# A weight decoding shared out anew: 16-bit copies on ScalarE, the first rescaling on GpSimd

## The chip, the cores and the metric

The kernel runs on one core of a Trainium2 chip. Its time is the device time of one launch in microseconds (us), the median of several runs; less is better. A core has five engines with queues of their own: TensorE (matrix products, PE in the rows), VectorE (DVE), ScalarE (ACT), GpSimd (POOL) and SyncE (SP, which here issues the DMA transfers). Each engine takes its instructions strictly in the order in which the program lists them; between engines they wait for each other by semaphores.

## The reference

Attention with normalized queries and keys, and then a feed-forward part. Inputs and the weights are drawn in NumPy: q, k, v are float32, the weights come to the kernel as float64.

```python
def _attn_ref(q, k, v, g_q, g_k):            # q, k, v: (8, 12, 448, 64)
    q_n, k_n = rmsnorm(q, g_q), rmsnorm(k, g_k)
    scores = matmul(q_n, k_n.T) / sqrt(64)
    attn = softmax(scores)                   # with 1e-9 added to the sum
    return matmul(attn, v)

def _moe_ref(x, w_in, w_out):                # x: (3584, 768), w_in: 768 x 2048
    h = x @ w_in
    g = h * np.cos(h)
    return g @ w_out                         # w_out: 2048 x 768
```

## The kernel before

The kernel has two parts. The first does all the attention, two heads at a time (48 units `u`, six of them to each of the 8 batches), and between the units' instructions the products `h = x @ w_in` of the batches already done. The second part does the last products of this kind, the cosine and the product with `w_out`. All products are made in float32 precision from a high and a low part of each operand; the first six units alone are "plain", that is, they use float32 products without such parts.

The 16 blocks of `w_in` (one for each 128 of the 2048 hidden columns, 128x768 numbers each) arrive as float64, 768 KB each, by DMA (`w_load`, L254). The chip doesn't compute in float64, so each is decoded in place. The 64-bit numbers are seen as pairs of 32-bit words; the upper word (`up`) holds sign, exponent and the first 20 bits of the mantissa, the lower word the other 32, of which float32 still takes 3. `decode` (L259 to L270) does this in four steps:

- step 0, ScalarE (L263): the upper words, read as float32, are multiplied by 2 to the power of -112 into a buffer `f`, which corrects the exponent;
- step 1, ScalarE (L266): the highest byte of each lower word is copied over the lowest byte of the upper word;
- step 2, VectorE (L268): the upper word is shifted right arithmetically by 5, and sign and three lowest bits are kept;
- step 3, VectorE (L270): `f` is shifted left by 3 as an integer, and combined with the upper word by "or".

Then ScalarE makes the high part (`w_high`, L280) and VectorE the low part, in two halves (`w_low`, L285). For the buffer `f` the blocks take turns between two places, `wf` and `aq`. A block's decoding needs the place that the block before the last has left.

The weights `w_out` go the same way in 32 quarters of 128x384 (`v_fetch`, `v_decode`), between about 180 and 860 us. Their seven combinations are stored in DRAM for the second part.

Other names in the rows: `score_plain` (L551) and `score` (L567) make the scores `S`; `rowmin` (L571, VectorE) scales them and finds their extreme; `expo` (L579, ScalarE) makes the probabilities `P`; `transp` (L613 to L622) transposes them on TensorE into PSUM `PT`; `pt_copy` (L668, L670) copies `PT` to SBUF for the plain units, `pt_high` and `pt_low` (L636, L643, L645) make its high and low part for the others; `av` (L660, L662) and `av_plain` (L678 to L688) multiply by v. On GpSimd are the powers for the norms (`st_pow`, L398, L399), the scaling of keys (`k_norm`, L473, L476) and queries (`q_scale`, L492), the low parts of both (`k_low`, L482, `q_low`, L498), v's parts (L522, L526), the division by the sum (`x_norm`, L717) and the low part of x (`x_split`, L728). `ffn1` (L744 to L746) makes the first product of the feed-forward part.

The order of the instructions isn't written by hand. Each piece of work is given by `add` an engine, a cost and a due time, and what it reads and writes. `Plan.order` then walks through time with these costs: an engine that is free takes, of the pieces that are ready, the one due first. The resulting list is emitted as it is. The due times are corrected by tables of numbers: `SHIFT` (by function and stage), `PAIR` (by unit), `BEGIN` (the earliest start of loads) and some terms in the number of the block. After that `hold` moves the pieces named in `YIELD` behind a key's normalization where one follows within 4 us, in the first 60 us.

Of the kernel before, what the change touches and what calls it, by code (L numbers as in the profile page):

```python
# [13 lines left out]
U8 = mybir.dt.uint8  # L14
# [11 lines left out]
class Plan:  # L26
# [123 lines left out]
    YIELD, AHEAD, WITHIN, UNTIL = ("x_norm", "w_low"), "k_norm", 4.0, 60.0  # L150
# [20 lines left out]
def tile_attention_moe(  # L171
# [14 lines left out]
    NP = NU // B  # L186
    NQT = 7
# [158 lines left out]
    kboth, qlow = {}, [apool.tile([128, 768], F32R, tag="E0", name="E0", bufs=1)]  # L346
# [18 lines left out]
    def e_clear(i):  # L365
        if i:
            qlow.append(apool.tile([128, 768], F32R, tag="E1", name="E1", bufs=1))
# [85 lines left out]
    def rkb(u):  # L453
        return (qtwo[u % 2][:, :S] if u < NP else kboth[u % 2][:, S:]).bitcast(F32)

# [3 lines left out]
    def rk_load(u):  # L459
        if u < NP + 2:  # L460
# [10 lines left out]
    def k_norm(u):  # L471
        if u >= NP:
# [11 lines left out]
    def q_plain(u):  # L484
        return q6[:, u]
# [4 lines left out]
    def q_scale(u):  # L490
        q = q_plain(u) if u < NP else qd
        nc.gpsimd.tensor_scalar(q, q, gsc[u < NP], 0.0, op0=ALU.mult, op1=ALU.add)  # L492

# [35 lines left out]
    def place(u, n):  # L529
        i = 7 * min(u, NP) + (n if u < NP else 0)  # L530
        if u < NP:
            return ("ph", i // 4) if i % 4 == 3 else ("S", 3 * (i // 4) + i % 4)
        return ("S", i - i // 4 + 7 * (u - NP) + n)

    NSP = 7 * NP // 4
# [72 lines left out]
    def transp(u, kc, part, last):  # L608
# [5 lines left out]
        else:  # L614
# [4 lines left out]
            c, n = (k - 64, 128) if u < NP else (k, 64)  # L619
# [215 lines left out]
    def y_store(b, oc, src):  # L835
# [5 lines left out]
        "av": (5.3, 39.33, 0.0), "av3": (-13.83, 15.47, 0.0), "av_plain": (0.0, 0.0, 10.94),  # L841
        "d_place": (7.71, -0.4, 0.0), "e_clear": (2.06, 0.0, 0.0), "e_place": (-13.2, 0.0, 0.0),
        "expo": (7.95, 14.26, -11.58), "ffn1": (-3.18, -2.89, 0.0), "g_fold": (0.0, 0.0, 3.13),
        "g_load": (0.0, 0.0, 0.98), "h_both": (-29.07, 0.0, 0.0), "h_out": (-14.91, 5.31, 0.0),
        "h_store": (-0.09, 0.0, 0.0), "k_high": (7.68, 8.19, 0.0), "k_load": (0.0, 0.0, 1.22),
        "k_low": (33.26, 1.74, 0.0), "k_norm": (45.02, 0.0, -0.54), "kn_copy": (0.0, 0.0, -13.33),
        "kn_load": (0.0, 0.0, -45.16), "kn_norm": (0.0, 0.0, -20.32), "kn_pow": (0.0, 0.0, 29.13),
        "kn_reduce": (0.0, 0.0, -2.77), "kn_square": (0.0, 0.0, -6.31), "kn_turn": (0.0, 0.0, 1.63),
        "kq_load": (-17.42, -14.74, 0.0), "m_place": (-18.39, 4.08, 0.0), "pt_copy0": (0.0, 0.0, -3.9),
        "pt_copy1": (0.0, 0.0, -44.97), "pt_high0": (-25.09, -5.18, 0.0), "pt_high1": (-9.32, -33.28, 0.0),  # L850
        "pt_low0": (-20.85, 10.99, 0.0), "pt_low1": (-5.79, -41.16, 0.0), "q_high": (-79.7, 2.11, 0.0),
        "q_load": (0.0, 0.0, 5.21), "q_low": (-2.0, 3.7, 0.0), "q_scale": (-57.44, -11.45, -3.1),
# [12 lines left out]
    }
    PAIR = (18.33, 10.11, -12.21, 0.63, 7.01, 13.7, -4.94, -21.21, -1.78, 0.0, -39.42, -0.16)
# [487 lines left out]
```

## Time and profile before

| | |
|---|---|
| median of 3 runs | 1362.52 us (1362.02 to 1363.71) |
| the profiled execution, time | 1365.0 us |
| its span, first to last instruction | 1363.2 us |
| TensorE busy | 1339.7 us, 98% |
| VectorE, ScalarE, GpSimd busy | 74%, 72%, 42% |
| mean granted clock of TensorE | 0.996 |

Rows of the profile give an engine, a line of the kernel, an operation with its output and inputs, and times. In a timeline a row is the start, the duration, the engine, the line, the operation and its operands with their shapes, and in brackets how long the engine stood idle before it, and what released it. PE's durations overlap, since products are pipelined: the distance between two starts tells what one costs. A wait that has several causes is put down to the one that came last.

### The profile page before, as it was taken

The numbers are of one execution on the slowest core, as the hardware profiler recorded it, in microseconds if no ns is written. First come the engines' busy times: TensorE is split into PE (matmuls) and PEld (weight loads), VectorE is DVE, ScalarE is ACT, GpSimd is POOL, SyncE is SP. The second block draws the span as 40 slices with busy tenths as digits, with TensorE's granted clock in tenths as the row PEclk, the third lists the DMA queues.
The fourth block names the chain that finished last, engine by engine and source line by source line (L and its number), as shares of the span: only waits on it lengthen the run. The fifth ranks groups of instructions, "written<-read, shape, count | busy, mean of one in ns | idle before, by whom it ended". The sixth has DMA issues, their size and how long they took to land.

```text
span 1363.2 us, 21477 instructions
## 1 busy us (share of the span) xinstructions
PE 1339.7 (98%) x6998; PEld 1173.4 (86%) x6998; DVE 1013.0 (74%) x1795; ACT 977.6 (72%) x1920; POOL 579.1 (42%) x522
## 2 busy tenths in 40 slices
PE   6998999999999999999999999999999999999998
PEld 3447888988989899899898889999999999999998
DVE  5988887677777767677767776518889889889743
ACT  7999988787887888787887787646566366366321
POOL 4576657676765866765765675310000000000000
PEclk9998999999999999999999999999999999999999
DMA  6998879889898898898888878248989369369334
GB/s 209 263 286 221 178 192 236 227 240 245 237 234 219 216 245 222 212 256 227 215 221 229 219 208 225 88 176 278 332 287 311 111 246 315 107 246 316 104 113 153
DMA packets 149472, 302.19 MB, mean 222 GB/s; under 512 B 34368, under 2 KB 83088, under 8 KB 149360
## 3 DMA queue, kind: packets, MB, share of 16 engines
q1 hardware_dynamic: 149360, 300.83, 76.8%
q8 instruction: 55, 0.90, 0.3%
q14 instruction: 57, 0.47, 0.1%
HBM read 193.99 MB, written 62.73 MB: 188 GB/s over the span
## 4 chain that ended last, share of the span: by engine, by line
PE 87%; ACT 5%; DVE 3%; POOL 2%; issue 2%; DMA 1%; SPq 0%; ACTq 0%; POOLq 0%; DVEq 0%
PE y L819 10%; PE y L818 10%; PE y L820 10%; PE ph L744 9%; PE ph L745 9%; PE ph L746 9%; PE S L567 8%; PE PT L613 7%; PE O L660 5%; PE O L662 3%; ACT P L579 1%; PE y L746 1%; PE y L744 1%; PE y L745 1%; PE PT L618 1%
## 5 line engine op out<-in xcount | busy, mean ns | idle before, releaser
L571 DVE TENSOR_SCALAR_CACHE_REDUCE S<-S,r 128x448 f32<-128x448 f32 x336 | 224.8, 686 | 59.4 <-PE S L567 49.6
L744 PE MATMUL ph<-xs,wi 128*128 128x448 f32 x660 | 250.7, 380 | 0.2 <-ACT hbuf L762 0.2
L819 PE MATMUL y<-g,wo 128*128 128x448 f32 x672 | 245.4, 365 | 0.0
L818 PE MATMUL y<-g,wo 128*128 128x448 f32 x672 | 245.4, 365 | 0.0
L820 PE MATMUL y<-g,wo 128*128 128x448 f32 x672 | 245.4, 365 | 0.0
L745 PE MATMUL ph<-xs,wi 128*128 128x448 f32 x660 | 242.2, 367 | 0.0
L746 PE MATMUL ph<-xs,wi 128*128 128x448 f32 x660 | 241.4, 366 | 0.0
L579 ACT ACTIVATE P<-S,sm 128x448 f32<-128x448 f32 x336 | 214.4, 644 | 26.2 <-DVE S L571 23.7
L800 ACT CAST g<-gq 128x896 fp32r<-128x896 f32 x112 | 105.7, 943 | 172.8 <-PE y L820 172.3
L636 ACT CAST hi<-PT 128x512 fp32r<-128x512 f32 (+1 forms) x336 | 172.5, 538 | 73.1 <-PE PT L620 42.9
L643 DVE TENSOR_TENSOR lo<-PT,hi 128x512 fp32r<-128x512 f32 x252 | 151.4, 617 | 49.3 <-ACT hi L636 48.7
L798 DVE TENSOR_TENSOR g<-gq,g 128x896 fp32r<-128x896 f32 x112 | 122.0, 1089 | 61.5 <-ACT g L800 61.1
L613 PEld LDWEIGHTS PT<-ident,P 128*128 128x128 f32 x1008 | 120.7, 140 | 37.0 <-ACT hi L670 6.0
L613 PE MATMUL PT<-ident,P 128*128 128x128 f32 x1008 | 146.2, 274 | 1.8 <-DVE lo L643 1.5
L744 PEld LDWEIGHTS ph<-xs,wi 128*128 128x128 f32 x660 | 124.4, 188 | 13.9 <-ACT hbuf L762 1.4
L819 PEld LDWEIGHTS y<-g,wo 128*128 128x128 f32 x672 | 126.2, 188 | 10.0
L820 PEld LDWEIGHTS y<-g,wo 128*128 128x128 f32 x672 | 126.2, 188 | 10.0
L818 PEld LDWEIGHTS y<-g,wo 128*128 128x128 f32 x672 | 126.2, 188 | 10.0
L746 PEld LDWEIGHTS ph<-xs,wi 128*128 128x128 f32 x660 | 124.2, 188 | 10.7
L745 PEld LDWEIGHTS ph<-xs,wi 128*128 128x128 f32 x660 | 124.7, 189 | 8.7
L399 POOL TENSOR_TENSOR r<-r,nhalf 128x14 f32<-128x14 f32 (+1 forms) x48 | 122.6, 2554 | 4.0
L660 PE MATMUL O<-hi,vs 128*128 128x448 f32 x336 | 118.7, 370 | 0.0
(125 smaller groups left out, 2588.4 us busy)
## 6 DMA issues: line engine op xcount, KB each, us to landing
wo<-wo_d SPq DMA_DIRECT2D x152, 384.0 KB
gq<-h_d SPq DMA_DIRECT2D x64, 448.0 KB
h_d<-hbuf SPq DMA_DIRECT2D x54, 448.0 KB
wo_d<-ao SPq DMA_DIRECT2D x56, 384.0 KB
sd<-sd SPq DMA_DIRECT2D x46, 448.0 KB
kq<-kq SPq DMA_DIRECT2D x42, 480.0 KB
D<-qhi SPq DMA_DIRECT2D x84, 192.0 KB
raw<-w_in SPq DMA_DIRECT2D x16, 768.0 KB
```

The costliest lines, as they stand in the source:

```text
L571: nc.vector.tensor_scalar(d["S", t][:, :S], d["S", t][:, :S], d["r"][:, t : t + 1], None, op0=ALU.mult, op1=ALU.min, accum_out=d["sm"][:, ...
L579: nc.scalar.activation(p_rows(u, t), d.pop(("S", t))[:, :S], AF.Exp, bias=sm[:, 1, t : t + 1], scale=-1.0, accum_out=sm[:, 2, t : t + 1],)
L613: nc.tensor.transpose(pt[part][:, i * 128 : i * 128 + 128], p_rows(u, t)[:, c : c + 128], ident)
L636: nc.scalar.copy(hi if kc < 3 else hi[:64], pt_rows(u, kc, part))
L643: nc.vector.tensor_tensor(lo, src, hi.bitcast(F32), ALU.subtract)
L660: nc.tensor.matmul(O, st, d["hi", kc][:, HEADS[hh]], start=(kc == 0), stop=(kc == 3))
L744: nc.tensor.matmul(ph[:, :S], whi, x2[:, 0, :], start=(cc == 0), stop=False)
L745: nc.tensor.matmul(ph[:, :S], whi, x2[:, 1, :], start=False, stop=False)
L746: nc.tensor.matmul(ph[:, :S], wlo, x2[:, 0, :], start=False, stop=(cc == NCC - 1))
L818: nc.tensor.matmul(y, whi, hi[:, e], start=first and e == 0, stop=False, **more)
L819: nc.tensor.matmul(y, whi, lo[:, e], start=False, stop=False, **more)
L820: nc.tensor.matmul(y, wlo, hi[:, e], start=False, stop=last and e == NG - 1, **more)
```

## The change

- Step 1 of the decoding copies 16 bits for 8: the upper half of the lower word over the lower half of the upper word. Step 2 shifts by 13 instead of 5. This holds for both kinds of weights.
- Step 0 of `w_in`'s sixteen blocks goes from ScalarE to GpSimd (`w_rebias`, a product with 2 to the power of -112 and a sum with 0). For `w_out` step 0 stays on ScalarE.
- The costs that the planner assumes for step 3 and for `w_low` are changed (1.27 to 1.0, 0.53 to 0.6), and `w_low` no longer stands in `YIELD`.
- All the numbers in `SHIFT`, `PAIR` and `BEGIN` are new. New terms by number of block: -0.494 for -0.33 (`w_in`), 19.58 + 25.488 for 2.55 + 25.482 (`w_out`).
- A constant `NF` = 6 takes the place of `NP` = 6 and of literal numbers where the plain units are meant; the values are the same.

```diff
-    YIELD, AHEAD, WITHIN, UNTIL = ("x_norm", "w_low"), "k_norm", 4.0, 60.0
+    YIELD, AHEAD, WITHIN, UNTIL = ("x_norm",), "k_norm", 4.0, 60.0
...
         elif step == 1:
-            by = st.bitcast(U8).rearrange("p (n t) -> p n t", t=8)
-            nc.scalar.copy(by[:, :, 4], by[:, :, 3])
+            words = st.bitcast(U16).rearrange("p (n t) -> p n t", t=4)
+            nc.scalar.copy(words[:, :, 2], words[:, :, 1])
         elif step == 2:
-            nc.vector.tensor_scalar(up, up, 5, SIGN_LOW, op0=ALU.arith_shift_right, op1=ALU.bitwise_and)
+            nc.vector.tensor_scalar(up, up, 13, SIGN_LOW, op0=ALU.arith_shift_right, op1=ALU.bitwise_and)
...
+    def w_rebias(fc):
+        wfl[fc] = w_flat(fc)
+        up = raw[fc].bitcast(F32).rearrange("p (n t) -> p n t", t=2)[:, :, 1]
+        nc.gpsimd.tensor_scalar(wfl[fc], up, REBIAS, 0.0, op0=ALU.mult, op1=ALU.add)
+
     def w_decode(fc, step):
-        if step == 0:
-            wfl[fc] = w_flat(fc)
         decode(raw[fc], wfl[fc], step)
...
     SHIFT = {
...
-        "v_sum": (1.69, 0.0, 0.0), "w_decode": (70.22, 0.0, 0.0), "w_high": (3.68, 0.0, 0.0),
-        "w_load": (-3.56, 0.0, 0.0), "w_low": (2.76, 0.0, 0.0), "x_half": (-1.22, 1.78, 0.0),
...
+        "v_sum": (-17.09, 0.0, 0.0), "w_decode": (38.64, 0.0, 0.0), "w_load": (3.43, 0.0, 0.0),
+        "w_low": (7.04, 0.0, 0.0), "w_rebias": (2.77, 0.0, 0.0), "x_half": (7.15, -12.73, 0.0),
...
-    BEGIN = {"v_load": -5.46, "q_load": 4.31, "v_fetch": -9.59, "st_load": -5.63, "w_load": 12.81, "k_load": 10.48, "kq_load": -37.77, "v_plain": -2.91}
+    BEGIN = {"v_load": -9.1, "q_load": 4.47, "v_fetch": -39.58, "st_load": -4.95, "w_load": 12.86, "k_load": 15.5, "kq_load": -73.61, "v_plain": -0.99}
...
-        if name in ("w_load", "w_decode", "w_high", "w_low"):
-            due += -0.33 * first
+        if name in ("w_load", "w_rebias", "w_decode", "w_high", "w_low"):
+            due += -0.494 * first
...
-            late = BEGIN.get(name0, 0.0) + (0.075 * first if name0 == "w_load" else 0.0)
+            late = BEGIN.get(name0, 0.0) + (-0.001 * first if name0 == "w_load" else 0.0)
...
-            for step, eng, cost in ((0, ACT, 0.84), (1, ACT, 0.84), (2, DVE, 0.74), (3, DVE, 1.27)):
+            add(POOL, 1.0, d - 8.0, w_rebias, fc, r=[w], w=[f])
+            for step, eng, cost in ((1, ACT, 0.84), (2, DVE, 0.74), (3, DVE, 1.0)):
                 add(eng, cost, d - 8.0 + step, w_decode, fc, step,
-                    r=[w] if step in (0, 3) else [], w=[f] if step in (0, 3) else [w])
+                    r=[w] if step == 3 else [], w=[f if step == 3 else w])
...
-            add(DVE, 0.53, d, w_low, fc, hf, nc.vector, r=[f, w], w=[("wlo", fc, hf)])
+            add(DVE, 0.6, d, w_low, fc, hf, nc.vector, r=[f, w], w=[("wlo", fc, hf)])
```

## Rows read from the trace of the kernel before

**Rows 1.** The page's first part: busy time, share of the span, instructions, by engine

```profile
PE 1339.7 (98%) x6998; PEld 1173.4 (86%) x6998; DVE 1013.0 (74%) x1795; ACT 977.6 (72%) x1920; POOL 579.1 (42%) x522
```

**Rows 2.** Stretches: us, busy PE, PEld, DVE, ACT, POOL, then clock, DMA share, GB/s

```profile
100.00:110.00 10.00, 10.00 (x52) 6.72 (x51) 7.82 (x19) 9.70 (x20) 9.64 (x9) 1.00 1.05 294
110.00:120.00 10.00, 6.19 (x28) 4.77 (x28) 10.00 (x18) 9.56 (x20) 6.35 (x7) 0.79 1.08 255
...
20.00:180.00 160.00, 151.85 (x736) 97.89 (x737) 140.64 (x294) 150.13 (x295) 99.79 (x84) 0.98 0.89 237
...
260.00:1000.00 740.00, 739.61 (x4033) 668.24 (x4032) 521.78 (x1056) 564.16 (x1235) 413.76 (x374) 1.00 0.83 227
```

**Rows 3.** Waits of TensorE, 0 to 20 us: total us, times, longest

```profile
PE PT L438 <- DVE kq L433: 8.0, 1, 8.0
```

**Rows 4.** Waits of TensorE, 20 to 260 us

```profile
PE PT L618 <- DVE lo L643: 2.7, 1, 2.7
PE S L567 <- ACT P L579: 2.6, 3, 1.1
PE O L678 <- ACT hi L670: 2.1, 2, 1.1
PE PT L613 <- DVE lo L643: 1.5, 2, 0.8
PE S L551 <- ACT P L579: 1.1, 1, 1.1
```

**Rows 5.** Timeline of TensorE: start, us, line, operation, idle before and releaser

```profile
69.52 1.02 PE L551 MATMUL S<-km,q 128*128 128x448 f32 x2 [1.13 <-ACT P L579]
...
107.53 0.37 PE L744 MATMUL ph<-xs,wi 128*128 128x448 f32 x1
107.73 0.37 PE L745 MATMUL ph<-xs,wi 128*128 128x448 f32 x1
...
117.04 0.90 PE L618 MATMUL PT<-ident,P 128*128 128x128 f32 x3 [2.72 <-DVE lo L643]
...
118.70 0.57 PE L567 MATMUL S<-M,D 128*128 128x448 f32 x1
...
122.44 0.43 PE L745 MATMUL ph<-xs,wi 128*128 128x448 f32 x1
```

**Rows 6.** Timeline of ScalarE, 66 to 69 us

```profile
66.11 0.92 ACT L263 ACTIVATE aq<-raw 128x768 f32<-128x768 f32 x1 [1.16 <-issue]
67.06 1.96 ACT L266 COPY raw<-raw 128x768 uint8<-128x768 uint8 x1
```

**Rows 7.** Timeline of VectorE, at 63 and 107 us

```profile
63.40 0.55 DVE L285 TENSOR_TENSOR wi<-aq,wi 128x384 fp32r<-128x384 f32 x1
...
107.75 0.88 DVE L268 TENSOR_SCALAR raw<-raw 128x768 int32<-128x768 int32 x1 [1.45 <-ACT raw L266]
```

**Rows 8.** Tile raw: count, ns least/median/most, first and last start

```profile
L266 ACT COPY raw<-raw x16: 1907/1980/2091, 26.9 to 174.6; 128x768 uint8<-128x768 uint8 x16
...
L263 ACT ACTIVATE wf<-raw x8: 895/912/939, 25.5 to 165.3; 128x768 f32<-128x768 f32 x8
```

**Rows 9.** Tile rawo, a quarter of w_out

```profile
L266 ACT COPY rawo<-rawo x32: 1063/1080/1128, 190.4 to 860.6; 128x384 uint8<-128x384 uint8 x32
```

**Rows 10.** GpSimd by line and shape, 20 to 260 us: busy us, mean ns, idle before

```profile
L492 POOL TENSOR_SCALAR kq<-kq,gs 128x512 f32<-128x512 f32 x11 | 9.0, 814 | 6.9 <-DMA kq<-kq 6.9
L522 POOL TENSOR_SCALAR vs<-vd 128x512 fp32r<-128x512 f32 x10 | 6.3, 635 | 10.9 <-PE O L660 9.4 <-DMA vd<-v 1.5
L398 POOL TENSOR_SCALAR r<-r 128x14 f32<-128x14 f32 x15 | 4.7, 316 | 39.8 <-DVE r L393 39.6
```

**Rows 11.** All engines by line and shape, 0 to 200 us: w_low

```profile
L285 DVE TENSOR_TENSOR wi<-aq,wi 128x384 fp32r<-128x384 f32 x16 | 12.2, 786 | 0.4 <-ACT wi L280 0.3
L285 DVE TENSOR_TENSOR wi<-wf,wi 128x384 fp32r<-128x384 f32 x16 | 11.8, 769 | 0.6 <-ACT wi L280 0.6
```

More of the change, by code (lines that the diff above doesn't have):

```diff
@@ L13 @@
 I32 = mybir.dt.int32
-U8 = mybir.dt.uint8
+U16 = mybir.dt.uint16
 AF = mybir.ActivationFunctionType
@@ L186, in tile_attention_moe @@
     NP = NU // B
+    NF = 6
     NQT = 7
@@ L345, in tile_attention_moe @@
     KHOME = (0, 1, 2, 3, 4, 2)
-    kboth, qlow = {}, [apool.tile([128, 768], F32R, tag="E0", name="E0", bufs=1)]
+    kboth, qlow = {}, {}
     kq = apool.tile([128, S + 512], F32, tag="kq", name="kq", bufs=1)
@@ L365, in e_clear @@
     def e_clear(i):
-        if i:
-            qlow.append(apool.tile([128, 768], F32R, tag="E1", name="E1", bufs=1))
+        i = (NF + i) % 2
+        qlow[i] = apool.tile([128, 768], F32R, tag=f"E{i}", name=f"E{i}", bufs=1)
         nc.vector.tensor_scalar(
@@ L490, in q_scale @@
     def q_scale(u):
-        q = q_plain(u) if u < NP else qd
-        nc.gpsimd.tensor_scalar(q, q, gsc[u < NP], 0.0, op0=ALU.mult, op1=ALU.add)
+        q = q_plain(u) if u < NF else qd
+        nc.gpsimd.tensor_scalar(q, q, gsc[u < NF], 0.0, op0=ALU.mult, op1=ALU.add)
     def q_high(u):
@@ L529, in place @@
     def place(u, n):
-        i = 7 * min(u, NP) + (n if u < NP else 0)
-        if u < NP:
+        i = 7 * min(u, NF) + (n if u < NF else 0)
+        if u < NF:
             return ("ph", i // 4) if i % 4 == 3 else ("S", 3 * (i // 4) + i % 4)
-        return ("S", i - i // 4 + 7 * (u - NP) + n)
-    NSP = 7 * NP // 4
+        return ("S", i - i // 4 + 7 * (u - NF) + n)
+    NSP = 7 * NF // 4
     def score_plain(u, j):
@@ new lines, in tile_attention_moe @@
+        "ffn1": (-0.45, -3.23, 0.0), "g_load": (0.0, 0.0, 2.04), "h_both": (-14.26, 5.1, 0.0),
+        "h_out": (-12.49, 20.6, 0.0), "h_store": (2.07, 0.0, 0.0), "k_high": (10.35, 8.91, 0.0),
+        "k_low": (0.0, 11.42, 0.0), "k_norm": (58.53, 12.98, 2.31), "kn_copy": (0.0, 0.0, -0.84),
+        "kn_load": (0.0, 0.0, -28.91), "kn_norm": (0.0, 0.0, -0.93), "kn_pow": (0.0, 0.0, -0.07),
+        "kn_reduce": (0.0, 0.0, -3.51), "kn_square": (0.0, 0.0, -6.43), "kn_turn": (0.0, 0.0, 1.16),
+        "kq_load": (-20.41, -9.87, 0.0), "m_place": (27.69, 12.35, 0.0), "pt_copy0": (0.0, 0.0, -25.15),
@@ new lines, in tile_attention_moe @@
+        "pt_copy1": (0.0, 0.0, -67.76), "pt_high0": (-79.14, 41.7, 0.0), "pt_high1": (-6.74, -88.69, 0.0),
+        "pt_low0": (-24.23, 14.64, 0.0), "pt_low1": (27.75, 0.0, 0.0), "q_high": (-26.14, -6.02, 0.0),
+        "q_load": (0.0, 0.0, -0.09), "q_low": (-21.14, 2.75, 0.0), "q_scale": (-15.34, -4.21, 0.0),
+        "rk_load": (-17.86, 46.7, 0.0), "rk_spread": (0.0, 0.0, -3.79), "rowmin": (29.01, 67.9, 39.75),
+        "rs_copy": (5.99, 2.21, 3.92), "rs_load": (-3.46, 2.74, -26.9), "rs_store": (-13.25, 0.0, 4.69),
@@ new lines, in tile_attention_moe @@
+        "rsum": (5.13, -0.28, -0.33), "score": (0.0, -1.1, 0.0), "score_plain": (0.0, 0.0, -0.81),
+        "st_load": (8.97, 2.87, -1.4), "st_pow": (-19.93, 0.0, -1.56), "st_reduce": (37.79, -10.99, 16.99),
+        "st_square": (-0.1, -2.26, -2.95), "st_store": (15.14, 61.57, 3.04), "transp0": (-17.17, -38.32, -35.38),
+        "transp1": (3.55, -11.36, 0.0), "v_decode": (-43.76, 0.0, 0.0), "v_fetch": (-1.76, 0.0, 0.0),
+        "v_high": (0.0, 12.8, 0.0), "v_load": (-26.43, 2.23, 0.0), "v_low": (-91.11, -3.63, 0.0),
@@ L875, in add @@
         elif name[:2] not in ("w_", "v_", "e_") or name in ("v_load", "v_high", "v_low", "v_plain", "e_place"):
-            stage = 2 if first < NP else int(first < NP + 3)
+            stage = 2 if first < NF else int(first < NF + 3)
         if name in ("pt_low", "pt_high", "pt_copy", "transp"):
@@ L881, in add @@
         due += SHIFT.get(name, (0.0,) * 3)[stage]
-        if name in ("w_load", "w_decode", "w_high", "w_low"):
-            due += -0.33 * first
+        if name in ("w_load", "w_rebias", "w_decode", "w_high", "w_low"):
+            due += -0.494 * first
         if name in ("ffn1", "h_out", "h_store", "h_both") and not first:
-            due += -0.23 * args[1]
+            due += -0.328 * args[1]
         if name in ("v_fetch", "v_decode", "v_sum", "v_split", "v_store"):
-            due += 2.55 + 25.482 * first
+            due += 19.58 + 25.488 * first
         other = ("w_load", "w_decode", "w_high", "w_low", "v_fetch", "v_decode", "v_sum", "v_split", "v_store", "e_clear")
@@ L990, in prepare @@
             add(SP, ISS, D0 - 34, kq_load, u, w=kd + qd, kb=480.0, start=D0 - 40)
-        add(SP, ISS, D0 - 45, st_load, u, w=sd, kb=224.0 if turned else 448.0, start=0.0 if u < NP else D0 - 60)
+        add(SP, ISS, D0 - 45, st_load, u, w=sd, kb=224.0 if turned else 448.0, start=0.0 if u < NF else D0 - 60)
         if plain:
@@ L1164, in tile_attention_moe @@
             for i in range(RING["E"]):
-                add(DVE, 0.56, 24.0 + 45 * i, e_clear, i, w=[("E0", i)] + [("km", 4)] * i + [("E", NP + i)], start=20.0)
+                add(DVE, 0.56, 24.0 + 45 * i, e_clear, i, w=[("E0", i)] + [("km", 4)] * (i * (NF > 5)) + [("E", NF + i)], start=20.0)
         multiply(b, NFC if b < B - 1 else NEAR)
```

47 lines of the change are left out of this document (15 added, 32 removed).

## Prediction

> **What bounds the kernel now.** I began with the busy shares of the whole span: TensorE is busy 1339.7 us of 1363.2, 98% [rows 1]. A change on the other engines can therefore give back at most the 23.5 us in which TensorE is idle, and whatever it loses to a lower clock. Next I read the stretches, to see where those 23.5 us lie. From 260 to 1000 us TensorE is busy 739.61 of 740 us [rows 2]. That stage is closed: work saved there on another engine can't show. From 20 to 180 us TensorE is busy 151.85 of 160 us, while ScalarE is busy 150.13, VectorE 140.64 and GpSimd 99.79 [rows 2]. So the place to look is the first 260 us, and in it two engines stand almost as full as TensorE.
>
> TensorE's own waits from 20 to 260 us name the culprits: 2.6 + 2.1 + 1.1 = 5.8 us end with ScalarE (exponentials and PSUM copies), and 2.7 + 1.5 = 4.2 us end with VectorE's low part of the probabilities: 10.0 us in all [rows 4]. The opening 8.0 us, in which TensorE waits for the first normalized k, are outside this [rows 3]. The last few microseconds, the output store behind the last product, are untouched too.
>
> One of those waits costs more than itself. After the 2.72 us wait that ends at 117.04, ten matmuls begin between 118.70 and 122.44, 0.374 us apart, against 0.20 at 107.53 [rows 5]; the mean granted clock of 110 to 120 us is 0.79 [rows 2], so part of this stretch ran at the lower level, 1.2 GHz. It lasts about 5.4 us (117.04 to 122.44), of which 5.4 x (1 - 0.20/0.374) = 2.5 us are lost. What could be removed in all between 20 and 260 us is then 10.0 + 2.5 = 12.5 us.
>
> Last I read what stood on ScalarE ahead of such a wait. The exponential for which TensorE stands still until 69.52 [rows 5] came directly behind a rescaling (66.11, 0.92 us) and a byte copy (67.06, 1.96 us) [rows 6]. Three further waits on ScalarE have the same pair, or one of the two, a few instructions ahead of them: those that end near 32, 90 and 114 us. The 2.72 us wait goes the same way around a corner: VectorE stood idle 1.45 us for the byte copy at 107.75, with the two-part subtraction for which TensorE waited still queued behind [rows 7].
>
> **The change part by part.**
>
> *The rescaling leaves ScalarE.* Sixteen of 0.91 us [rows 8]: 16 x 0.91 = 14.6 us less between 25 and 175 us. ScalarE goes from 150.1 to about 135.5 of 160 us.
>
> *The copy moves 16 bits for 8.* The byte copy takes 1.98 us for 768 elements, over twice the float32 rescaling of the same count and the same 8-byte step on its input (0.91) [rows 8], and the 384-element copy takes 1.08 [rows 9]. No row shows a 16-bit copy. Upper bound: it stays at 1.98, if what is slow is a store of part of a word. Lower bound: 0.9, if only single bytes are slow. I take 0.95, since all wider rows of ScalarE lie there; that would save 16 x 1.03 = 16.5 us in the first stage, and nothing at the upper bound. The Trainium skill (ScalarE: Activation LUTs, section What ACT_TABLE_LOAD costs) gives 186 ns + 0.833 ns per element for every function, float32 and bf16 alike, which would be an estimated 0.83 us here. The float32 row is near it, the byte row is not, so the page has no word on bytes, and by it the saving would be 18.4 us instead of 16.5.
>
> The 32 later copies (384 elements) would save up to 32 x 0.55 = 17.6 us of ScalarE after 180 us. All but the first few lie in the stage in which TensorE waits for nothing, so I cost them at zero; what covers them is the full TensorE of [rows 2].
>
> *GpSimd takes the rescaling.* The nearest rows: one-input operations on 128x512 take 0.81 (q scaled) or 0.64 us (v copied), on 128x14 0.32 [rows 10]. Scaled from 512 to 768 elements: 0.64 x 1.5 = 0.96 and 0.81 x 1.5 = 1.2. The 8-byte step on the input has no row on this engine; if it doubled the cost, 2.4. I take 1.1, so 16 x 1.1 = 17.6 us more, GpSimd from 99.8 to 117 of 160 us. Most of GpSimd's idle time in there is waiting for VectorE's reductions, so the total fits. Not so near 100 to 110 us, where it is busy 9.64 of 10 [rows 2].
>
> *A new wait.* The 16-bit copy overwrites what GpSimd reads, so on ScalarE it now waits for GpSimd's rescaling. Behind it in ScalarE's queue are the exponentials and the PSUM copies, on which TensorE waits at once. Where GpSimd is on time it costs nothing; where it is late it costs up to one rescaling, 1.1 us. A rescaling in turn waits for the load and for the buffer of the block before last, and behind it on GpSimd stand the key's normalization, q's and k's low parts, and x's low part.
>
> *Collisions of GpSimd and VectorE.* The low part of the weights (32 subtractions with two SBUF inputs) takes 12.2 + 11.8 = 24.0 us; its short case is 0.55, which would be 17.6 [rows 7, 11]. The 6.4 us between them arise beside 99.8 us of GpSimd work; 17.6 us more would add 1.1 us in proportion, and with the integer operations of the decoding about twice that: 2 us on VectorE.
>
> *Due times anew.* They reorder every queue. The starts of the weight loads stay (12.86 for 12.81 us added to each, and the 0.075 us per block gone), so no weight lands over 1.1 us earlier. The decoding is due 32 us earlier (38.64 for 70.22) and 0.16 us more per block; the rescaling, with 2.77, ahead of it. Dropping the low part of the weights from the operations held back until a key's normalization only moves VectorE's work by up to 4 us; but for the rescaling two blocks on, whose buffer it frees, nobody waits for it before the first feed-forward product, near 106 us. The start can't shorten: load, square, sum, power, scaling and transposition follow one another for the first 8 us [rows 3]. The order of TensorE's own work can move the end a little each way: I allow 2 us.
>
> *The sum.* Of the 12.5 us, those that stand behind a byte copy or a rescaling: 2.1 (the two on the copy of the probabilities, near 32 and 90) + 1.1 (near 69) + 1.1 (the longest of the three before the later scores, near 114) = 4.3 [rows 4], plus 2.7 + 2.5 for the wait at 117 and its clock: 9.5 us. Taken off: the 2 us that VectorE loses to GpSimd, and 1.5 us for rescalings that come late at the new wait, one wholly and part of a second, which is my choice between none and all sixteen: 6.0 us remain. The profiled execution goes from 1365.0 (span 1363.2, 1.8 around it) to 1359.0. It lay 2.5 above the median of 1362.52, so on the median: **1356.5 us**.
>
> **The rivals.**
>
> *The copy remains slow (the change does half of what it says).* Then ScalarE saves 14.6 us, not 31. The waits shrink only where a rescaling stood ahead (near 32, 69 and 114) and the wait at 117 shrinks by the 0.92 us before it: 3.2 + 0.9 + about half of the clock's 2.5, less the same 3.5 given back: about 2 us, 1360.5. For it: nothing in the trace shows a narrow store that is fast. Chance 0.15.
>
> *VectorE becomes the bound.* If each rescaling holds up a two-input operation for its whole length, VectorE goes from 140.6 to 158 of 160 us. Then the waits on ScalarE (5.8 us) go, but those on VectorE double (4.2 + 2.5 more): 1362.5 - 5.8 + 6.7 = 1363.4, no change. Against it: the two-input rows of today are lengthened by 6.4 us beside 99.8 us of GpSimd work, not by all of it. Chance 0.1. The Trainium skill (SBUF — State Buffer, section Summary: rules for kernel authors) speaks for this rival: beside a VectorE operation with two SBUF inputs, the second of the two engines to issue blocks until the first is done. The lengthened rows agree in kind.
>
> *GpSimd's queue delays the second part's start (slower).* Between 90 and 110 us GpSimd has no room. If four rescalings fall there ahead of q's, k's and x's low parts, scores and first products come 4 x 1.1 = 4.4 us later, TensorE falls to the lower clock again (what it costs today, 2.5, is not won), and the four waits on ScalarE are half won (2.1), with the wait at 117 staying: 1362.5 + 4.4 + 1.2 for a longer stretch at that clock - 2.1 = 1366. It decides from the point at which the new wait exceeds what TensorE has queued in that stretch, about 2 us. For it: the decoding is now due earlier, and rescalings no longer sit where the order had slack. Chance 0.2.
>
> *Everything goes.* All 12.5 us and nothing given back: 1350. Chance 0.12.
>
> **How the numbers follow.** Forecast (1353 to 1359.5): 0.43. Some 0.2%, 2.7 us, is what a measurement of this kernel can tell from no change. The slow copy's case lies on that edge (1359.8), and I put two thirds of it on the side of no change. Faster: 0.43 + 0.12 + 0.05 = 0.60. Within 0.2%: 0.10 + 0.10 = 0.20. Slower: 0.20. The range runs from 1350 (all of it) to 1366 (the rival on GpSimd), which leaves about one in ten out on either side.
>
> **What would show it.** The copy's row at about 0.95 us for 768 elements and 0.5 for 384; rescalings on GpSimd at about 1.1; ScalarE from 150 to some 118 us busy between 20 and 180 us; TensorE's waits from 20 to 260 us at 3 to 5 us, with no stretch at the lower clock after 20 us. I am wrong if ScalarE's copy waits for GpSimd by more than 2 us in sum with TensorE behind it, if VectorE's two-input rows grow by more than 5 us, or if TensorE's busy time itself differs by more than 3 us, which would be its order and not the decoding.

## The result: 0.58% slower, and the profile after

| | before | after |
|---|---|---|
| median | 1362.27 us (1361.33 to 1363.71, 4 runs) | 1372.06 us (1370.83 to 1374.41, 4 runs) |
| ratio, with its 95% interval | | 1.0058 [1.0042, 1.0074] |
| profiled execution, span | 1363.2 us | 1370.2 us (its time 1372.19) |

The forecast was 1356.5 us in a range up to 1366. The changed kernel came out slower than before and outside the range: the medians lie 9.8 us apart, the ratio with its interval makes it 7.9 us. Measured again beside other kernels (e11_after_again, below) it stood at 1.0080 [1.0064, 1.0096], 10.9 us. Where a run below is compared with the changed kernel, both ratios are used.

Busy time by engine of the whole span, after (it answers to [rows 1]):

```profile
PE 1345.2 (98%) x6998; PEld 1172.8 (86%) x6998; DVE 1018.6 (74%) x1795; ACT 969.5 (71%) x1904; POOL 595.5 (43%) x538
```

ScalarE lost only 8 us of work and GpSimd gained 16: the rescaling moved (16 instructions), and the copy got no shorter, as the tiles of the weights say. Columns: count, ns least/median/most, first and last start (it answers to [rows 8, 9]):

```profile
L267 ACT COPY raw<-raw x16: 1942/1976/2084, 26.8 to 167.2; 128x768 uint16<-128x768 uint16 x16
...
L276 POOL TENSOR_SCALAR wf<-raw x8: 881/906/1621, 23.8 to 156.8; 128x768 f32<-128x768 f32 x8
L276 POOL TENSOR_SCALAR aq<-raw x8: 875/887/1222, 28.3 to 166.2; 128x768 f32<-128x768 f32 x8
...
L267 ACT COPY rawo<-rawo x32: 1066/1081/1109, 184.4 to 872.6; 128x384 uint16<-128x384 uint16 x32
```

The 16-bit copy takes 1.976 us where the byte copy took 1.980; GpSimd's rescaling is short, 0.89 to 0.91 us. Now the stretches, first of before and then of after. Columns: us, busy PE (records), PEld, DVE, ACT, POOL, then clock, DMA share, GB/s:

```profile
100.00:140.00 40.00, 35.82 (x179) 28.48 (x178) 34.25 (x70) 37.31 (x74) 27.55 (x24) 0.91 0.89 221
700.00:750.00 50.00, 50.00 (x277) 44.92 (x277) 37.72 (x81) 40.57 (x93) 31.56 (x29) 1.00 0.82 225
```

```profile
20.00:180.00 160.00, 150.62 (x707) 93.71 (x706) 138.40 (x290) 137.02 (x275) 112.98 (x97) 0.97 0.86 231
100.00:140.00 40.00, 34.31 (x160) 25.59 (x159) 30.25 (x64) 33.25 (x64) 29.11 (x24) 0.87 0.86 211
120.00:130.00 10.00, 8.26 (x25) 6.17 (x26) 6.61 (x13) 7.11 (x16) 6.72 (x6) 0.58 0.71 123
260.00:1000.00 740.00, 737.14 (x4016) 663.43 (x4015) 520.71 (x1047) 564.20 (x1234) 414.23 (x375) 1.00 0.81 223
700.00:750.00 50.00, 48.08 (x267) 42.68 (x266) 33.73 (x74) 37.29 (x85) 26.48 (x27) 1.00 0.87 235
```

Both traces hold 6998 products of TensorE, so the number of products begun in a stretch is a ledger of where the time went, and a better one than busy shares. Between 100 and 140 us after has 160 of them, before 179; at 0.205 us each (the spacing in [rows 5]) the 19 missing ones are about 3.9 us. Between 700 and 750 us it has 267 for 277: another 2.0 us. These two places hold some 5.9 of the 7.0 us between the spans. It is an estimate, since transpositions are cheaper than 0.205. Some of what is missing at 180 us is made good by 260; there after has begun 1176 products, before 1193, and from 260 to 750 us it loses as many again (2697 for 2716). From 20 to 180 us TensorE, VectorE and ScalarE have all become less busy than before [rows 2]; only GpSimd has gained. The freed time went idle.

**The first place, 115 to 132 us.** Waits of TensorE from 20 to 260 us, after (total, times, longest):

```profile
PE S L571 <- ACT P L583: 4.0, 3, 2.9
PE PT L617 <- ACT hi L674: 2.2, 3, 1.2
PE ph L748 <- ACT hbuf L766: 1.2, 1, 1.2
PE PT L617 <- DVE lo L647: 0.9, 2, 0.6
```

All of them with the four smaller ones make 9.8 us; before it was 10.0 [rows 4]. The waits on VectorE's low part went from 4.2 to 0.9, and a new wait of 2.9 on the exponential came in their stead. Here it is, in the timelines of GpSimd, ScalarE and TensorE:

```profile
114.83 0.89 POOL L276 TENSOR_SCALAR aq<-raw 128x768 f32<-128x768 f32 x1
115.69 0.88 POOL L276 TENSOR_SCALAR wf<-raw 128x768 f32<-128x768 f32 x1
```

```profile
115.75 3.76 ACT L267 COPY raw<-raw 128x768 uint16<-128x768 uint16 x2 [0.42 <-POOL aq L276]
119.14 0.74 ACT L583 ACTIVATE P<-S,sm 128x448 f32<-128x448 f32 x1
```

```profile
120.02 0.47 PE L571 MATMUL S<-khi,qhi 128*128 128x448 f32 x1 [2.92 <-ACT P L583]
...
123.33 0.74 PE L749 MATMUL ph<-xs,wi 128*128 128x448 f32 x1 [0.37 <-POOL xs L732]
...
125.67 0.74 PE L748 MATMUL ph<-xs,wi 128*128 128x448 f32 x1 [1.23 <-ACT hbuf L766]
126.21 0.57 PE L749 MATMUL ph<-xs,wi 128*128 128x448 f32 x1
126.58 0.57 PE L750 MATMUL ph<-xs,wi 128*128 128x448 f32 x1
...
131.88 0.36 PE L748 MATMUL ph<-xs,wi 128*128 128x448 f32 x1
132.09 0.37 PE L749 MATMUL ph<-xs,wi 128*128 128x448 f32 x1
```

The new order has two rescalings and behind them the copies of blocks 9 and 10 in one run: 3.76 us on ScalarE, and behind them three exponentials, for the first of which TensorE stands still 2.92 us. The planner counts 0.86 us for a copy, the chip takes 1.9. After the wait products begin 0.37 us apart (126.21, 126.58) until 131.9, where they are again 0.21 apart: the lower level of 1.2 GHz lasts from about 121.3 to 131.9, with 1.6 us of waits inside it. The 9.0 us that it ran lost by estimate 9.0 x (1 - 0.205/0.373) = 4.0 us, against 2.5 before. Blocks 9 and 10 weren't urgent: TensorE takes the sixteen blocks in turn, and hadn't finished the first; its product is the one copied to `hbuf` at 125.08.

**The second place, 710 us**, where before waits for nothing. ScalarE, GpSimd and TensorE, after:

```profile
710.26 0.62 ACT L499 CAST qhi<-kq 128x512 fp32r<-128x512 f32 x1 [2.69 <-POOL kq L496]
```

```profile
709.53 0.70 POOL L496 TENSOR_SCALAR kq<-kq,gs 128x512 f32<-128x512 f32 x1 [9.09 <-DMA kq<-kq]
```

```profile
712.79 0.33 PE L617 MATMUL PT<-ident,P 128*128 128x128 f32 x1 [1.38 <-DVE xf L718]
...
714.08 0.47 PE L748 MATMUL ph<-xs,wi 128*128 128x448 f32 x1 [0.54 <-ACT hbuf L766]
```

A load of queries lands late, GpSimd and then ScalarE wait for it in order, and what stands behind comes late to TensorE: 1.9 us. No part of the decoding of `w_in` is in this chain, and its last copy starts at 167.2: what differs here is the order that the new due times give.

### The profile page after: what moved, and what is told of

It reads as the page before. It is cut to its first block, busy times and chain, and to the rows that moved or that the text cites. A ratio compares the mean times of both kernels' runs of the same rounds, so it can differ in the third digit from the quotient of the medians.

```text
span 1370.2 us, 21522 instructions
## 1 busy us (share of the span) xinstructions
PE 1345.2 (98%) x6998; PEld 1172.8 (86%) x6998; DVE 1018.6 (74%) x1795; ACT 969.5 (71%) x1904; POOL 595.5 (43%) x538
## 4 chain that ended last, share of the span: by engine, by line
PE 90%; ACT 3%; DMA 3%; DVE 2%; POOL 1%; issue 1%; SPq 0%; POOLq 0%; ACTq 0%
PE y L822 10%; PE y L824 10%; PE y L823 10%; PE ph L748 9%; PE ph L749 9%; PE ph L750 9%; PE S L571 8%; PE PT L617 7%; PE O L664 5%; PE O L666 3%; PE S L555 1%; PE y L749 1%; PE y L750 1%; PE y L748 1%; PE PT L622 1%; ACT raw L267 1%
## 5 line engine op out<-in xcount | busy, mean ns | idle before, releaser
L640 ACT CAST hi<-PT 128x512 fp32r<-128x512 f32 (+2 forms) x336 | 176.7, 537 | 36.6 <-PE PT L617 14.1
L647 DVE TENSOR_TENSOR lo<-PT,hi 128x512 fp32r<-128x512 f32 (+1 forms) x252 | 151.9, 616 | 38.2 <-ACT hi L640 36.5
L617 PE MATMUL PT<-ident,P 128*128 128x128 f32 x1008 | 153.6, 275 | 6.3 <-ACT hi L674 2.2
L750 PEld LDWEIGHTS ph<-xs,wi 128*128 128x128 f32 x660 | 124.8, 189 | 10.9
L664 PE MATMUL O<-hi,vs 128*128 128x448 f32 x336 | 124.8, 383 | 0.0
```

Source lines behind the costliest of these rows:

```text
L617: nc.tensor.transpose(pt[part][:, i * 128 : i * 128 + 128], p_rows(u, t)[:, c : c + 128], ident)
L640: nc.scalar.copy(hi if kc < 3 else hi[:64], pt_rows(u, kc, part))
L647: nc.vector.tensor_tensor(lo, src, hi.bitcast(F32), ALU.subtract)
L664: nc.tensor.matmul(O, st, d["hi", kc][:, HEADS[hh]], start=(kc == 0), stop=(kc == 3))
L750: nc.tensor.matmul(ph[:, :S], wlo, x2[:, 0, :], start=False, stop=(cc == NCC - 1))
```

## The experiments

Ratios are against the kernel before on the same chip.

**Each part of the change alone.** First the width of the copy, in the order of before:

```diff
-            by = st.bitcast(U8).rearrange("p (n t) -> p n t", t=8)
-            nc.scalar.copy(by[:, :, 4], by[:, :, 3])
+            words = st.bitcast(U16).rearrange("p (n t) -> p n t", t=4)
+            nc.scalar.copy(words[:, :, 2], words[:, :, 1])
...
```

> The kernel before with the 16-bit copy and the shift by 13, nothing else; the order of all queues stays. If the width of the copy is neither gain nor loss (the copy took 1.98 us for 768 elements at 8 bits and 1.98 at 16 bits in the two profiles), the time stays within 0.1% of the kernel before, 1362.3, and the copy's row reads 1.9 to 2.0 us. If the wide copy has a part in the loss, the time rises by several us.

1364.22 us, 1.0003 [0.9993, 1.0012]; the copy's median is 1974 ns. The width does nothing, as expected. Why, a run with 16 more copies of 768 elements shows; they stand at the start of ScalarE's work, in eight forms (float32 or 16 bits, with a step of 8 bytes or none on either side), two of each:

```diff
...
+        for dst, src in pairs:
+            for _ in range(2):
+                nc.scalar.copy(dst, src)
```

> The kernel before with sixteen copies of 768 elements added ahead of it on ScalarE, eight forms twice: float32 and 16 bits, with and without a step of 8 bytes on either side. If the narrow type is slow by itself, the 16-bit copy without a step takes about 1.98 us. If a store with a step is slow, float32 with a step on the output takes it too. If only a narrow store with a step is, the four float32 forms and the two 16-bit forms that write without a step stay at 0.8 to 0.95 us.

Rows of ScalarE's timeline: a float32 store with a step; 16 bits without a step; a step on the input alone; on the output alone; on both; 16 bits to float32.

```profile
10.26 0.87 ACT L859 COPY P<-P 128x768 f32<-128x768 f32 x1
...
12.58 0.83 ACT L859 COPY P<-P 128x768 uint16<-128x768 uint16 x1
...
15.22 0.88 ACT L859 COPY P<-P 128x768 uint16<-128x768 uint16 x1
16.12 1.89 ACT L859 COPY P<-P 128x768 uint16<-128x768 uint16 x1
...
21.89 1.89 ACT L859 COPY P<-P 128x768 uint16<-128x768 uint16 x1
...
23.81 0.88 ACT L859 CAST P<-P 128x768 f32<-128x768 uint16 x1
```

Only a 16-bit store with a step is slow, 1.89 us; the 16-bit read with a step takes 0.88, the float32 store with a step 0.87. This was the case behind the prediction's upper bound ("if what is slow is a store of part of a word"), and a 16-bit copy keeps that store. (A byte copy without a step wasn't run.)

Then the move to GpSimd alone and the due times alone, each planned anew. The first adds `w_rebias` to before with the old due times; the second puts step 0 of the changed kernel back on ScalarE:

```diff
...
-            for step, eng, cost in ((0, ACT, 0.84), (1, ACT, 0.84), (2, DVE, 0.74), (3, DVE, 1.27)):
+            add(POOL, 1.0, d - 8.0, w_rebias, fc, r=[w], w=[f])
+            for step, eng, cost in ((1, ACT, 0.84), (2, DVE, 0.74), (3, DVE, 1.27)):
...
```

> The kernel before with the rescaling on GpSimd and byte copies, all due times as before (the rescaling takes over the due time of its old step). Theory 1, the new due times made the loss: the sixteen rescalings off ScalarE shorten the waits behind it, 1356 to 1362. Theory 2, the handover between GpSimd and ScalarE made it: 1367 to 1372, with ScalarE's copies waiting for GpSimd.

```diff
-            add(POOL, 1.0, d - 8.0, w_rebias, fc, r=[w], w=[f])
+            for step, eng, cost in ((0, ACT, 0.84), (1, ACT, 0.84), (2, DVE, 0.74), (3, DVE, 1.0)):
...
```

> The kernel after with the rescaling back on ScalarE, right before its copy, with the new due times and the wide copy. Theory 1, the due times made the loss: 1370 to 1376, as ScalarE bears 14.6 us more as well. Theory 2, the handover made it: about 1362.

1390.48 us, 1.0194 [1.0176, 1.0212], and 1381.01 us, 1.0123 [1.0108, 1.0139]. Neither time lies in a range that its two theories gave, and either part without the other is worse than both together. The parts aren't additive, since a replanned order is another kernel. So the next runs keep an order and change one thing in it.

**The move in a fixed order.** In the order of before, step 0 is issued on GpSimd at the place where ScalarE had it:

```diff
+        if step == 0:
...
+            nc.gpsimd.tensor_scalar(wfl[fc], up, REBIAS, 0.0, op0=ALU.mult, op1=ALU.add)
```

> The kernel before with the rescaling on GpSimd, emitted at the very place in the list where it stood for ScalarE; nothing is planned anew, so all other queues keep their order, and GpSimd's gets sixteen more. Theory 1 (the loss comes from the order, not from the handover): 1356 to 1362, as 14.6 us leave ScalarE. Theory 2 (the handover and GpSimd's queue cost): 1366 or more, with ScalarE's copies waiting for GpSimd.

1367.9 us, 1.0033 [1.002, 1.0046], as the second theory said: 4.5 us slower, with 14 us less work on ScalarE between 20 and 180 us (135.8 for 150.1). Waits of ScalarE from 20 to 180 us, one of them in its timeline, and TensorE behind it:

```profile
ACT raw L266 <- POOL aq L277: 7.9, 4, 3.3
ACT raw L266 <- POOL wf L277: 3.4, 3, 1.5
```

```profile
111.12 1.99 ACT L266 COPY raw<-raw 128x768 uint8<-128x768 uint8 x1 [3.26 <-POOL aq L277]
```

```profile
115.41 0.47 PE L571 MATMUL S<-M,D 128*128 128x448 f32 x1 [2.10 <-ACT P L583]
```

The copy waits 11.3 us for GpSimd, seven times. Now the mirror of it: the changed kernel in its own order, with step 0 issued on ScalarE at GpSimd's place.

```diff
-        nc.gpsimd.tensor_scalar(wfl[fc], up, REBIAS, 0.0, op0=ALU.mult, op1=ALU.add)
+        nc.scalar.activation(wfl[fc], up, AF.Copy, scale=REBIAS)
```

> The changed kernel in its own order, with step 0 of the sixteen blocks emitted on ScalarE where GpSimd had it. ScalarE then has some 15 us more in 20 to 180 us (137 to about 152), and the copy no longer waits for GpSimd. Theory (the new order is made for a ScalarE that is relieved, so the move to GpSimd and the new times belong together): 4 to 10 us slower than the changed kernel, about 1376 to 1382. Rival (the handover to GpSimd itself costs, as it did by 4.5 us in the order of before): 2 to 5 us faster than the changed kernel, about 1367 to 1370.

1379.14 us, 1.0111 [1.0093, 1.013], slower than the changed kernel by 0.0111 less 0.0058 or 0.0080, that is 4 to 7 us, as the theory said. The new order is made for the move: there the move gains about what it lost in the old one. The likely reason, which wasn't tried by itself, is that the copies stand later behind their rescalings (they wait 2.0 us in sum in the changed kernel). The row in front of the longest stall of this run shows the same place with a rescaling added to its load:

```profile
120.97 0.94 ACT L276 ACTIVATE wf<-raw 128x768 f32<-128x768 f32 x1
121.77 3.77 ACT L267 COPY raw<-raw 128x768 uint16<-128x768 uint16 x2
```

```profile
126.05 0.71 PE L571 MATMUL S<-khi,qhi 128*128 128x448 f32 x1 [3.16 <-ACT P L583]
```

**The length of the copy in either order.** All 16 copies cut to 64 of 768 elements (0.34 us each), in before and in the changed kernel, and in the latter also to 300 elements, which is the length that the planner assumes (0.87 us measured). The edit is shown for the changed kernel, with n = 64 or 300; before has the same in its byte copy:

```diff
-            nc.scalar.copy(words[:, :, 2], words[:, :, 1])
+            nc.scalar.copy(words[:, :n, 2], words[:, :n, 1])
...
```

> The kernel before, its order kept, with all sixteen copies of the first weights cut from 768 to 64 elements (the lowest bits of most of these weights are left wrong), so about 0.3 us each instead of 1.98: some 27 us less on ScalarE before 175 us, about as much as the forecast took off it. If the waits that stand behind copies and rescalings are worth what the forecast summed (9.5 us, less what is given back), the time falls by 4 to 9 us, to 1355 to 1359. If freed time on ScalarE only lets another wait end last, it falls by under 2 us.

> The kernel after, its order kept, with all sixteen copies of the first weights cut to 64 elements (the lowest bits of most of these weights are left wrong). If the copy's true length (1.98 us where the planner counted 0.86) is what breaks this order before 140 us, the time falls by 3 to 6 us, to 1366 to 1369, and what is left lies after 260 us (2.4 us near 712).

> The changed kernel with each of the 16 copies cut to 300 of 768 elements, which leaves the low bits of the other elements wrong; by the length of the rows it then takes about 0.86 us, what the planner assumes for it. Theory (the copies' true length is the smaller part of the loss in this order, the order itself keeps 3 to 4 us): 1364.5 to 1368, ratio 1.0015 to 1.004. Rival (the new order is good, if only the copy were as short as it was planned): at most 1361, a ratio under 0.999.

| copy | order of before | order of after |
|---|---|---|
| 1.98 us | 1 | 1.0058 and 1.0080 |
| 0.87 us | | 1.0017 [1.0007, 1.0027] |
| 0.34 us | 0.9979 [0.9969, 0.9989] | 1.0011 [1.0000, 1.0022] |

Before gained less than the 4 to 9 us that were expected, the changed kernel (1365.39 us) somewhat more than its 3 to 6, and with 0.87 us (1366.71) it came where the theory had it. Three things follow. With 26 us of copies gone, the order of before gains 2.9 us: ScalarE's load was worth little. The true length of the copy costs the new order 5.6 to 8.6 us (1.0058 or 1.0080 less 1.0017), more than it was worth in the old: an order planned for 0.86 us has no room for 1.98. And with equally short copies the new order still loses 0.0032, 4.4 us, to the old. The two traces with copies of 0.34 us show where, first before and then the changed kernel (columns as in the stretches above):

```profile
0.00:260.00 260.00, 243.69 (x1222) 176.54 (x1223) 215.00 (x456) 211.39 (x485) 171.31 (x152) 0.99 0.87 230
260.00:750.00 490.00, 489.66 (x2716) 440.25 (x2715) 357.96 (x782) 399.24 (x915) 331.63 (x298) 1.00 0.89 231
```

```profile
0.00:260.00 260.00, 244.52 (x1230) 175.92 (x1231) 218.30 (x463) 203.47 (x477) 189.63 (x170) 1.00 0.86 237
260.00:750.00 490.00, 486.43 (x2686) 434.00 (x2685) 353.29 (x766) 393.59 (x903) 326.92 (x295) 1.00 0.86 223
```

Up to 260 us the new order with short copies is ahead, by 8 products. What it loses lies from 260 to 750 us: 30 products, by estimate up to 6 us at 0.2 each, and for 3.6 us TensorE stands idle. (Each trace is one execution.) No decoding of `w_in` is left there. With copies of 0.87 us it is the same: 1203 products up to 260 us, more than the 1193 of before, and 2701 for 2716 after that. So the long copies cost the new order its lead in the first 260 us, and its due times lose behind 260 us whatever the copy takes.

Before with short copies also tells on a wait that the prediction had counted on. TensorE's waits from 20 to 260 us, and ahead of the first of them ScalarE and VectorE:

```profile
PE PT L618 <- DVE lo L643: 2.6, 1, 2.6
PE S L567 <- ACT P L579: 2.0, 2, 1.2
```

```profile
108.41 0.62 ACT L495 CAST qhi<-kq 128x512 fp32r<-128x512 f32 x1 [3.04 <-POOL kq L492]
```

```profile
110.86 2.79 DVE L285 TENSOR_TENSOR wi<-wf,wi 128x384 fp32r<-128x384 f32 x2 [1.34 <-ACT wi L280]
```

The wait of 2.7 us at 117 [rows 4, 5] stays at 2.6 with copies of 0.34 us. What stood ahead of it on VectorE are two low parts of weights, 2.79 us, late because of ScalarE's high part of block 8. And ScalarE was late because it stood idle 3.04 us for GpSimd's scaling of the query: GpSimd is busy 9.87 of the 10 us from 100 to 110 in this run. The time taken off ScalarE there went into waiting for a third engine.

**Mending single places.** In the changed kernel the copies of blocks 9 and 10 alone cut to 64 elements:

```diff
-        decode(raw[fc], wfl[fc], step)
+        decode(raw[fc], wfl[fc], step, 64 if fc in (9, 10) else None)
...
```

> The kernel after, all queues in the same order; the copies of blocks 9 and 10 alone are cut from 768 to 64 elements, so the lowest bits of most of these two blocks' weights are left wrong. These are the two copies that stand back to back before three exponentials at 115.8 to 119.5 us, ahead of TensorE's wait of 2.92 us and its stretch at the lower clock. If this one place costs what the two traces differ by between 120 and 135 us, the time falls by 3 to 5.5 us, to 1366.5 to 1369, and the wait at 120 us and most of the lower clock go. If the lost time only moves on to the next wait, the time falls by less than 1.5 us.

1370.13 us, 1.0044 [1.0028, 1.0061]. The wait at 120 us is gone, a wait for `hbuf` at 126 has grown from 1.23 to 1.8, and one near 94 from 1.2 to 1.9. By the ratios it is 1.9 or 4.9 us under the changed kernel, depending on which of its two measurements is taken, so the run can't decide between its two theories. The same two copies whole, but moved behind the high part of x on ScalarE, with block 9's two steps on VectorE moved behind a row minimum, beside the changed kernel once more:

```diff
...
+        behind(("w_decode", 10, 1), ("x_split", 5, 0))
+        behind(("w_decode", 9, 1), ("x_split", 5, 0))
```

> The kernel after, whole computation; the two copies of blocks 9 and 10 go behind three exponentials on ScalarE, their two followers on VectorE behind one row minimum. If the two adjoining copies cost what they seem to (2.92 us of waiting and a longer stretch at the lower clock), the time falls by 3 to 5 us against the kernel after beside it. If the time moves on, by less than 1.5.

> The kernel after once more, beside the others on the same chip: 0.4 to 0.7% over the kernel before.

1371.79 us, 1.0061 [1.0048, 1.0074], against 1373.95, 1.0080 (just over the 0.7% expected), for the changed kernel beside it: 2 to 3 us less, between its two theories, with intervals that overlap. The exponentials are on time, but the copies now stand ahead of the copy of the first product (`hbuf`), which TensorE needs next. TensorE and ScalarE:

```profile
124.78 0.74 PE L760 MATMUL ph<-xs,wi 128*128 128x448 f32 x1 [5.26 <-ACT hbuf L778]
```

```profile
117.49 3.75 ACT L279 COPY raw<-raw 128x768 uint16<-128x768 uint16 x2
...
124.19 0.54 ACT L778 ACTIVATE hbuf<-ph 128x448 f32<-128x448 f32 x1
```

2.9 us of wait became one of 5.26. For the second place, two copies of x on ScalarE (`x_half`) were put ahead of the waiting `q_high`:

```diff
...
+                x = seq.pop([(x[2].__name__, x[3]) for x in seq].index(("x_half", (37, h))))
+                seq.insert([(x[2].__name__, x[3]) for x in seq].index(("q_high", (40,))), x)
```

> The kernel after; on ScalarE alone, the high part of unit 40's query goes behind the two copies of unit 37's output instead of ahead of them (it waits 2.69 us for a transfer at 707 to 710 us, and with it the transposition for which TensorE waits 1.38 us at 712.8). If that wait is lost time for good, the time falls by 1 to 2 us, to 1370 to 1371, and the row at 712 us loses its wait. If it moves on, nothing changes.

1371.08 us, 1.0053 [1.0036, 1.007]: the wait of 1.38 us went, 0.47 remained; TensorE has 271 products between 700 and 750 us in place of 267, under 1 us, and the time can't tell it from the changed kernel's. In the kernel before, the low part of block 8 and the shift of block 9 were put behind the low part of the probabilities for which TensorE stands still at 117:

```diff
...
+        behind(("w_decode", 9, 2), ("pt_low", 6, 2, 1))
+        behind(("w_low", 8, 1), ("pt_low", 6, 2, 1))
+        behind(("w_low", 8, 0), ("pt_low", 6, 2, 1))
```

> The kernel before, whole computation; on VectorE alone, three pieces of weight work (the low part of block 8's weights in two halves and the shift of block 9) go behind the low part of unit 6's probabilities, for which TensorE waits 2.7 us at 114 to 117 us. With the copies cut short that wait stayed (2.61 us), so the theory now is that VectorE's own queue makes it: 24 us beside GpSimd, not ScalarE's copy. Then the wait falls under 1 us, the stretch at the lower clock goes, and the time falls by 3 to 5 us, to 1358 to 1361. If ScalarE is what is late there, the wait stays above 2 us and the time within 1 us.

1363.39 us, 1.0000 [0.9991, 1.0009]: no gain where 3 to 5 us were expected. The stretch of 110 to 120 us keeps the full clock (1.00 for 0.79), but waits came elsewhere, and at the place itself 2.1 us remain. TensorE's waits from 20 to 260 us, and VectorE just ahead of the wait that remains (the profiled execution, 1367.18 us, is the slowest of its twelve):

```profile
PE S L578 <- ACT P L590: 3.4, 4, 1.3
...
PE PT L629 <- DVE lo L654: 2.1, 1, 2.1
```

```profile
117.24 1.16 DVE L654 TENSOR_TENSOR lo<-PT,hi 128x512 fp32r<-128x512 f32 x2 [3.03 <-ACT hi L647]
```

VectorE is free now, and stands idle 3.03 us for ScalarE's high part. That is the expectation's other case: ScalarE is late there as well. By these rows GpSimd, ScalarE and VectorE are late one behind the other at this wait, and relieving one of them left the next.

**A planner that knows the length.** Last, the changed kernel planned anew with 1.93 us for the copy:

```diff
-            for step, eng, cost in ((1, ACT, 0.84), (2, DVE, 0.74), (3, DVE, 1.0)):
+            for step, eng, cost in ((1, ACT, 1.93), (2, DVE, 0.74), (3, DVE, 1.0)):
```

> The changed kernel, but the planner is told 1.93 us for the copy in place of 0.84, and the order is planned anew with the same due times. Theory (due times fit one set of costs, and any other order made with them loses more than it mends): slower than before by 0.5 to 2 per cent, 1369 to 1390, though no two copies stand together ahead of an exponential near 116 us. Rival (the wrong length is the fault, and a planner that knows it mends the order): at most 1366.

1391.19 us, 1.0195 [1.0179, 1.0211], as the theory said. The right number makes it worse, by 16 or 19 us: these due times fit the costs that they were made with. Up to 180 us it isn't behind (715 products in 20 to 180 us, against 707 of the changed kernel), but from 260 to 1000 it is (3980 against 4016). Due times made anew for the true length weren't tried.

## Why the prediction was wrong, step by step

1. *"I take 0.95"* for the 16-bit copy failed. Measured: 1.976 us, the upper bound. The prediction had the right reason there, a store of part of a word, and chose the other end because "all wider rows lie there"; but the wider rows shown all wrote whole words. ScalarE's load fell to 137.0 us between 20 and 180, not 118.
2. *Rescaling on GpSimd at 1.1 us* was nearly right: 0.89 to 0.91, mean 0.93 to 0.99. GpSimd came to 113 us, forecast 117.
3. *The wait at 117 and its clock, 2.7 + 2.5 us, put down to the byte copy* failed. With copies of 0.34 us it stays. That VectorE had stood idle for a copy 9 us before the wait was a link in time, not the cause: with the copy short, ScalarE waits 3.04 us for GpSimd there. The prediction had read that GpSimd is busy 9.64 of the 10 us from 100 to 110, but hadn't put it into this chain. The removal of the copies gained 2.9 us in all, less than the 4.3 us that it had put on its other waits.
4. *The new wait at 1.5 us* was near for the new order, where ScalarE waits 2.0 us. In the old order it is 11.3 us, and the move costs 4.5 net.
5. *VectorE's loss beside GpSimd, 2 us,* didn't come in sum: VectorE's busy time between 20 and 180 us went from 140.6 to 138.4, the low part of the weights from 24.0 to 20.8 us (11.8 + 9.0), while the decoding's steps 2 and 3 rose from 27.6 to 31.3.
6. *The order, ±2 us,* is the term that decided. Even with a copy of 0.87 us, shorter than the 0.95 assumed, the changed kernel is 0.17% slower than before, not 0.44% faster. From the forecast's -6 us to the measured +7.9 or +10.9 (1.0058 or 1.0080) the length of the copy in this order makes up about 5.6 or 8.6 and the rest about 8.3: the overestimated gain and the order together. The order's own 4.4 us lie, by the traces with short copies, from 260 to 750 us, in the stage that the prediction called closed. That work saved there can't show was right, but the new due times reorder it too, and a stage without waits can only lose; it lost 30 products there with short copies, 19 in the changed kernel, the 2 us near 712 us among them. Which of the due times does it wasn't tried. One thing in the code was overlooked: the rescaling, unlike the other steps, also takes the term by number from `PAIR`, which moves two of the sixteen by more than 20 us ahead; it wasn't tried by itself.

The forecast had named three signs that it was wrong. TensorE's busy time differs by 5.5 us (1345.2 for 1339.7), over the 3 us that "would be its order and not the decoding": this one spoke. The copy's wait for GpSimd is at its limit of 2 us, and VectorE's two-input rows of the weights didn't grow in sum (24.0 + 16.0 us before, 20.8 + 18.0 after). The rival on a slow copy was right in its condition, but its 1360.5 presumed the old order. The rival on GpSimd's queue had the sign and, with 1366, the nearest number; that is luck in part, since its condition, a copy that waits more than 2 us for GpSimd near 110 us, is met in the order of before (e6: 3.26 us) and not in the changed kernel, where ScalarE's own two copies make the stall. The longer stretch at the lower clock came as it said, but the wait at 117, which it kept, went, and one at 120 took its place.

The later copies of `w_out` stayed at 1.08 us too, where 0.5 was forecast; their saving had been priced at nothing. The start (a first wait of 7.7 us for 8.0) is as forecast.

Not tried: a decoding whose step 1 stores whole words, which by estimate from the rows above could take 0.9 us.

## What to carry to other kernels

Where an order is planned from costs, price a change with the order that it brings: the same move of work cost 4.5 us in one order and gained 4 to 7 us in the other, and correcting one cost without the due times lost 16 or 19. Taking load off an engine that is 94% busy gave a tenth of it back: at the wait looked at, it then stood idle for the next engine in the chain, and a wait removed at one place came back at another. A stage in which the bounding engine waits for nothing can't win by less work elsewhere, but it can lose by a new order: look there too. Where the trace has no row for an operation, ask which property of the nearest slow row (width, step, side) the change keeps; here it kept the one that was slow.

## What the runs showed of the hardware

A copy on ScalarE that stores 8 or 16 bits with a step of 8 bytes takes 2.3 ns for an element (that the store and not the type is slow was tried with 16 bits alone): from the copies of 64, 300 and 768 elements (0.340, 0.872, 1.976 us) about 0.19 us stay fixed, and (1.976 - 0.340) / 704 = 2.32 ns come for each element. A 16-bit load with the same step, and a float32 store with it, cost 0.87 to 0.88 us for 768, hardly more than 0.83 without a step. The Trainium skill (ScalarE: Activation LUTs, section What ACT_TABLE_LOAD costs) gives 186 ns + 0.833 ns per element, an estimated 0.83 us for 768. The fixed part and all the other forms here agree (0.81 to 0.88 us), the narrow store with a step doesn't. On GpSimd a one-input product and sum over 768 float32 numbers with an 8-byte step on its input took 0.89 us in the median (up to 1.62), less than the 0.96 scaled from rows without a step.
